# Moving one step of a VectorE exponential chain to GpSimd, with a third buffer, a longer look-ahead and a re-planned fixed schedule

## The chip, the cores and the metric

The kernel runs on one core of one Trainium2 chip. The metric is the device time of that core in microseconds (us). Executions of one kernel agree within about 0.8%, mostly within 0.4%, so each time below is a median of several runs. Every timed kernel ran beside the kernel before on the same chip. A ratio is the mean time of one kernel's fast runs over that of the kernel before's fast runs of the same rounds, with a 95% interval, so it is not quite the ratio of the medians quoted.

## The reference, cut to what matters

Two layers, each multi-query attention followed by a gated MLP. S = 2048, D = 512, 32 heads of 16, one K and one V for all heads.

```python
def _A_ref(x, wq, wk, wv, wo):
    q = (x @ wq) -> 32 heads of 16;  k = x @ wk;  v = x @ wv
    scores = jnp.einsum('bhqd,bkd->bhqk', q, k) * Dh ** (-0.5)
    p = _softmax(scores, axis=-1)                 # 2 layers x 32 heads x 2048 x 2048 exponentials
    o = jnp.einsum('bhqk,bkd->bhqd', p, v)
    return o @ wo
...
for _ in range(2):                                # written out in the original
    x = x + _A_ref(_layernorm(x), ...)
    x = x + _B_ref(_layernorm(x), ...)            # gelu, layernorm, spatial 2048x2048 product, gate, w_out
```

The exponentials dominate: two layers make 4096 score blocks of 128x512.

## The kernel before

The program is a list scheduler that runs at build time. Each operation has a planned duration, and the scheduler places operations one after the other on five engines. What it emits is only the *order* of each engine, plus semaphore waits for the data dependences. The planned start times are not part of the program: an engine runs its list in order, as soon as the inputs of the next entry are there.

```python
def op(self, eng, fn, dur, deps=(), prio=5.0, ...):   # dur: planned us, used only at build time
...
def emit_program(nc, es, sched):
    for o in sched.commits:
        ...
        for d in sorted(o.deps, key=lambda d: -d.vis):
            if o.eng == "pe" and d.eng == "pe":
                continue
            ...
            waits.append((d.sem.h, d.val))            # waits for data, not for time
        def body(e, waits=waits, fn=o.fn, h=s.h, incv=incv):
            for (h_, v_) in waits:
                e.wait_ge(h_, v_)
            fn(e).then_inc(h, incv)
```

A score block goes one of two ways. "A" blocks are exponentiated by ScalarE straight from PSUM. "D" blocks go to VectorE in batches of two (1024 columns): one step from PSUM to int32 for each block, then six steps on the batch in SBUF. Which block goes where is decided while the schedule is built.

```python
# DexStream.take: may VectorE take another block now?
if not self.batch:
    self.open = [o for o in self.open if o.start is None or o.end > t]
    if len(self.open) >= 2:
        return None
    backlog = sc.free["dve"] - t + sum(o.dur for o in sc.ready["dve"] if ...)
    if backlog > BACKLOG:                             # 3.0 us
        return None
...
# DexStream.chain: the six steps of a batch after the PSUM step
o2 = sc.op("dve", ts(u, lo, 2.0 ** -16, None), d_sb(n, 0.521e-3), self.ops, pr)   # u16 low half -> fp16
o3 = sc.op("dve", ts(w, u, None, -1.0), d_sb(n, 0.26e-3), [o2, getattr(self, "wfree", None)], pr)
o4 = sc.op("dve", lambda e: e.tensor_tensor(q, u, w, ALU.mult), d_sb(n, 0.521e-3), [o3], pr)
self.wfree = o4
o5 = sc.op("dve", ts(u, u, C_B, C_A), d_sb(n, 0.26e-3), [o4], pr)
o6 = sc.op("dve", lambda e: e.tensor_tensor(q, q, u, ALU.mult), d_sb(n, 0.521e-3), [o5], pr)
o7 = sc.op("dve", lambda e: e.scalar_tensor_tensor(po.bitcast(U16), I, 2.0 ** -9, q, op0=ALU.mult, op1=ALU.add),
           d_sb(n, 1.042e-3), [o6] + self.war, pr)    # writes the bits of the bf16 result
```

TensorE has one queue in one fixed order: score matmuls for both kinds of blocks, value matmuls, projections, and warm-up matmuls on zeros that keep it busy.

The softmax here doesn't subtract the row's maximum and nothing guards it: scores larger than these inputs give would overflow.

## Time and profile before

| | before |
|---|---|
| median of three runs | 1871.99 us (1869.53 to 1872.58) |
| profiled span | 1867.6 us |
| blocks on VectorE / ScalarE | 501 / 3595 |
| mean granted TensorE clock | 0.990 |

The page of the kernel before, its line of busy time (engine, busy us, share of the span, instructions) and its line of the chain of work that ended last:

```profile
PE 1595.0 (85%) x11889; PEld 477.3 (26%) x11889; DVE 1736.9 (93%) x3107; ACT 1756.6 (94%) x1581; POOL 53.4 (3%) x94
...
ACT 36%; DVE 30%; PE 18%; issue 14%; POOL 1%; ACTq 0%; POOLq 0%; DVEq 0%
```

PE is TensorE, DVE is VectorE, ACT is ScalarE and POOL is GpSimd. ScalarE and VectorE are both nearly full, the last chain runs through both, and GpSimd is idle. The table of windows of the same kernel (window in us; its length; for each engine busy us and instructions; granted clock; DMA share; GB/s) confirms this for two steady stretches:

```profile
100.00:150.00 50.00, 39.52 (x311) 9.88 (x307) 49.49 (x84) 49.94 (x45) 0.00 (x0) 0.98 0.00 1
1000.00:1050.00 50.00, 39.75 (x322) 10.17 (x314) 48.96 (x82) 50.00 (x46) 0.00 (x0) 1.00 0.00 1
```

VectorE (third) has 49.0 to 49.5 of 50 us, and ScalarE (fourth) 49.9 to 50.0. The costliest groups of the same page (line, engine, operation, output and input with shapes, count; then busy us, mean ns of one; then idle us before them and what ended it):

```profile
L1343 ACT ACTIVATE Pa<-ps_all 128x1536 bf16<-128x1536 f32 (+1 forms) x1439 | 1637.5, 1368 | 31.1 <-PE ps_all L1615 16.2
...
L1520 DVE TENSOR_SCALAR E<-ps_all 128x512 int32<-128x512 f32 x501 | 341.1, 683 | 28.8 <-PE ps_all L1615 26.3
...
L1558 DVE SCALAR_TENSOR_TENSOR Pd<-E 128x1024 uint16<-128x1024 int32 x251 | 304.4, 1213 | 1.1
...
L1553 DVE TENSOR_TENSOR E<-E 128x1024 f16<-128x1024 f16 x251 | 171.3, 682 | 3.4
L1556 DVE TENSOR_TENSOR E<-E 128x1024 f16<-128x1024 f16 x251 | 171.0, 681 | 2.5
L1547 DVE TENSOR_SCALAR E<-E 128x1024 f16<-128x1024 uint16 x251 | 171.1, 682 | 1.6
L1549 DVE TENSOR_SCALAR E<-E 128x1024 f16<-128x1024 f16 x251 | 104.5, 416 | 2.2
L1550 DVE TENSOR_SCALAR E<-E 128x1024 f16<-128x1024 f16 x251 | 104.3, 415 | 2.3
```

L1520 is the PSUM step, L1547 the low-half step `o2`, L1549 and L1550 are `o3` and `o5`, L1553 and L1556 `o4` and `o6`, L1558 is `o7`. The low-half step is 171 us of a full VectorE. ScalarE waits for score matmuls for only 16.2 us.

### The profile page before, as it was taken

Reading aid. Unit: us, or ns where it says so; the run is one execution under the profiler, and the core shown is the slowest. Engines: PE = TensorE matmul, PEld = TensorE weight load, DVE = VectorE, ACT = ScalarE, POOL = GpSimd, SP = SyncE. Lnnn points to the kernel's source line nnn. Section 1 sums busy time; section 2 is a strip of 40 time slices with the busy share of each in tenths; the row PEclk is TensorE's granted clock in tenths of the full one; section 3 lists DMA queues with packets and bytes.
Section 4 is the critical chain, followed back from the end, with each engine's and each line's share of the span. In section 5 each row is a group of like instructions: output and inputs, shape, how many; then the busy total and the mean of one; then the engine's idle time right before and its main releaser. Section 6 shows DMA issues by size and latency. Waiting matters only on the chain.

```text
span 1867.6 us, 30386 instructions
## 1 busy us (share of the span) xinstructions
PE 1595.0 (85%) x11889; PEld 477.3 (26%) x11889; DVE 1736.9 (93%) x3107; ACT 1756.6 (94%) x1581; POOL 53.4 (3%) x94
## 2 busy tenths in 40 slices
PE   8777888878889988989887778887788799999898
PEld 3222222212222222223432122222222222222234
DVE  8999999999879999997889999999999689989978
ACT  8999999999989999998579999999999899999983
POOL 2000000000000000000100000000000000000000
PEclk9999999999989999999999999999999899999999
DMA  9700010000010020221210000000000100111213
GB/s 272 197 1 1 12 35 1 1 1 18 7 40 24 23 46 1 66 70 48 66 33 1 1 1 12 10 26 1 5 13 7 40 24 24 46 43 35 62 45 110
DMA packets 125142, 68.58 MB, mean 37 GB/s; under 512 B 79172, under 2 KB 121416, under 8 KB 125000
## 3 DMA queue, kind: packets, MB, share of 16 engines
q1 hardware_dynamic: 123416, 66.48, 13.2%
q8 instruction: 95, 1.56, 0.3%
q14 instruction: 47, 0.39, 0.1%
q10 hardware_dynamic: 1584, 0.16, 0.1%
HBM read 30.97 MB, written 17.83 MB: 26 GB/s over the span
## 4 chain that ended last, share of the span: by engine, by line
ACT 36%; DVE 30%; PE 18%; issue 14%; POOL 1%; ACTq 0%; POOLq 0%; DVEq 0%
ACT Pa L1343 34%; PE ps_all L1088 6%; PE ps_all L1615 5%; DVE E L1520 5%; DVE Pd L1558 4%; PE ps_all L1419 3%; DVE E L1556 2%; DVE E L1553 2%; DVE E L1547 2%; DVE gp L1100 2%; PE ps_all L1177 1%; DVE st L622 1%; DVE E L1550 1%; DVE E L1549 1%; DVE z2n L937 1%
## 5 line engine op out<-in xcount | busy, mean ns | idle before, releaser
L1343 ACT ACTIVATE Pa<-ps_all 128x1536 bf16<-128x1536 f32 (+1 forms) x1439 | 1637.5, 1368 | 31.1 <-PE ps_all L1615 16.2
L1615 PE MATMUL ps_all<-qs,kT 32*128 32x512 bf16 x4096 | 566.5, 387 | 226.3 <-ACT Pa L1343 206.6
L1520 DVE TENSOR_SCALAR E<-ps_all 128x512 int32<-128x512 f32 x501 | 341.1, 683 | 28.8 <-PE ps_all L1615 26.3
L1615 PEld LDWEIGHTS ps_all<-qs,kT 32*128 32x128 bf16 x4096 | 139.3, 91 | 779.3 <-ACT Pa L1343 728.7
L1419 PE MATMUL ps_all<-Pa,V 128*32 128x512 bf16 x3595 | 324.9, 388 | 1.5 <-DVE Pd L1558 0.6
L1558 DVE SCALAR_TENSOR_TENSOR Pd<-E 128x1024 uint16<-128x1024 int32 x251 | 304.4, 1213 | 1.1
L1601 PE MATMUL ps_all<-zero 128*128 128x512 bf16 x817 | 263.3, 393 | 2.1 <-POOL zero L585 1.0
L1088 PE MATMUL ps_all<-wsT,z2n 128*128 128x512 bf16 x714 | 199.0, 383 | 6.5 <-DVE E L1520 2.6
L1419 PE MATMUL ps_all<-Pd,V 128*32 128x512 bf16 x501 | 177.7, 389 | 0.0
L1553 DVE TENSOR_TENSOR E<-E 128x1024 f16<-128x1024 f16 x251 | 171.3, 682 | 3.4
L1556 DVE TENSOR_TENSOR E<-E 128x1024 f16<-128x1024 f16 x251 | 171.0, 681 | 2.5
L1547 DVE TENSOR_SCALAR E<-E 128x1024 f16<-128x1024 uint16 x251 | 171.1, 682 | 1.6
L1549 DVE TENSOR_SCALAR E<-E 128x1024 f16<-128x1024 f16 x251 | 104.5, 416 | 2.2
L1550 DVE TENSOR_SCALAR E<-E 128x1024 f16<-128x1024 f16 x251 | 104.3, 415 | 2.3
L1601 PEld LDWEIGHTS ps_all<-zero 128*128 128x128 bf16 x817 | 62.7, 98 | 138.0 <-issue 116.8
L1419 PEld LDWEIGHTS ps_all<-Pa,V 128*32 128x32 bf16 x3595 | 65.3, 94 | 125.4 <-issue 114.3
L1100 DVE TENSOR_TENSOR gp<-ps_all,gp 128x512 f16<-128x512 f32 x112 | 75.0, 682 | 21.8 <-PE ps_all L1088 21.8
L1088 PEld LDWEIGHTS ps_all<-wsT,z2n 128*128 128x128 bf16 x714 | 54.5, 97 | 105.2 <-issue 54.8
L784 PE MATMUL ps_all<-xnTA,wq_pad 128*128 128x512 bf16 (+2 forms) x384 | 72.4, 313 | 2.0 <-DVE qs L793 1.3
L962 PE MATMUL ps_all<-xnTB,w_in_r 128*128 128x512 bf16 (+2 forms) x336 | 62.6, 310 | 5.2 <-DVE z1s L973 2.3
L926 PE MATMUL ps_all<-w_in_r,xnTB 128*128 128x448 bf16 x256 | 63.4, 356 | 3.5 <-DVE z2n L937 1.4
L1177 PE MATMUL ps_all<-E 128*128 128x512 bf16 x224 | 53.6, 380 | 4.2 <-ACT E L1156 3.6
(87 smaller groups left out, 1013.9 us busy)
## 6 DMA issues: line engine op xcount, KB each, us to landing
wsT_scratch<-gp SPq DMA_DIRECT2D x16, 512.0 KB, 3.6
wsT<-wsT_scratch SPq DMA_DIRECT2D x8, 1024.0 KB, 5.4
z1s<-z_scratch SPq DMA_DIRECT2D x16, 448.0 KB, 3.8
wsT<-wsT_scratch SPq DMA_DIRECT2D x8, 512.0 KB, 3.4
z_scratch<-z1s SPq DMA_DIRECT2D x4, 896.0 KB, 5.2
X<-in_A_x_dram SPq DMA_DIRECT2D x8, 256.0 KB, 5.3
out_dram<-X SPq DMA_DIRECT2D x16, 128.0 KB, 1.9
w_in_r<-in_B_w_in_dram SPq DMA_DIRECT2D x1, 1792.0 KB, 10.3
```

The source lines that it names most:

```text
L1088: ins = e.matmul(self.b32(b), self.z2n[:, s, f * 128:(f + 1) * 128], w_[:, s - s0, :], start=st, stop=sp)
L1343: return e.activation(k.Pa[:, base:base + n, :], k.b32(b0, n).rearrange("p (k q) -> p k q", k=n), ACTF.Exp, scale=SCALE)
L1419: ins = e.matmul(k.b32(k.pvb)[32 * j:32 * j + 32, :], k.V[:, u.kt, 32 * j:32 * j + 32], b.slot, tile_position=(0, 32 * j), start=u.first, ...
L1520: return k.sc.op("dve", lambda e: e.tensor_scalar(k.eI[:, s, 512 * i:512 * (i + 1)], k.b32(j.bank.idx)[:, 0:512], C_LOG2, C_BIAS, op0=ALU. ...
L1547: return lambda e: e.tensor_scalar(out, a, m, None, op0=ALU.mult)
L1549: return lambda e: e.tensor_scalar(out, a, b, None, op0=ALU.add)
L1550: return lambda e: e.tensor_scalar(out, a, m, b, op0=ALU.mult, op1=ALU.add)
L1553: o4 = sc.op("dve", lambda e: e.tensor_tensor(q, u, w, ALU.mult), d_sb(n, 0.521e-3), [o3], pr)
L1556: o6 = sc.op("dve", lambda e: e.tensor_tensor(q, q, u, ALU.mult), d_sb(n, 0.521e-3), [o5], pr)
L1558: o7 = sc.op("dve", lambda e: e.scalar_tensor_tensor(po.bitcast(U16), I, 2.0 ** -9, q, op0=ALU.mult, op1=ALU.add), d_sb(n, 1.042e-3), [o6] ...
L1601: return e.matmul(k.b32(k.pvb if b is None else b.idx), k.zero[:], k.zero[:, None, :].to_broadcast([P, 4, P]), start=b is not None, stop=b ...
L1615: return e.matmul(self.b32(bank), self.kT[32 * j:32 * j + 32, kt * 128:(kt + 1) * 128], self.qs[32 * j:32 * j + 32, g.q.slot, :], tile_pos ...
```

## The change

Its intent: give the low-half step to the idle GpSimd, and use the VectorE time that comes free for more blocks. GpSimd and VectorE can block each other (in the trace after, a VectorE step of 0.42 us then takes 1.26), so the new planner keeps their steps apart in its plan ("lock"). A third set of buffers covers the longer chain.

```diff
-LOOK = 6
+LOOK = 8
+PATIENCE = 3.0
+POOL_FREE = 1.0
...
-NQS = 6
+NQS = 4
...
+NDB = 3
...
-        o2 = sc.op("dve", ts(u, lo, 2.0 ** -16, None), d_sb(n, 0.521e-3), self.ops, pr)
-        o3 = sc.op("dve", ts(w, u, None, -1.0), d_sb(n, 0.26e-3), [o2, getattr(self, "wfree", None)], pr)
-        o4 = sc.op("dve", lambda e: e.tensor_tensor(q, u, w, ALU.mult), d_sb(n, 0.521e-3), [o3], pr)
-        self.wfree = o4
+        o2 = sc.op("pool", ts(u, lo, 2.0 ** -16, None), n * 0.93e-3 + 0.2, self.ops + [self.end[s]], 2.0)
+        o3 = sc.op("dve", ts(q, u, None, -1.0), d_sb(n, 0.26e-3), [o2], pr)
+        o4 = sc.op("dve", lambda e: e.tensor_tensor(q, u, q, ALU.mult), d_sb(n, 0.521e-3), [o3], pr)
...
+        for o in (o2, o3, o4, o5, o6, o7):
+            o.lock = True
...
-            if len(self.open) >= 2:
+            if len(self.open) >= NDB:
...
+    def unlocked(self, o, t, eng):                 # earliest start of a "lock" operation in the plan
+        t = max(t, self.locked["pool" if eng == "dve" else "dve"])
+        if eng == "pool" and self.free["dve"] < o.ready + PATIENCE:
+            d = self.order["dve"][-1]
+            free = max(0.0, d.end - t) if not d.lock else 0.0
+            free += sum(x.dur for x in self.ready["dve"] if x.eng == "dve" and not x.lock and x.ready <= t)
+            if free < POOL_FREE:
+                return INF
+        return t
...
+        pace = []                                  # warm-up matmuls wait for a recent operation
+        if t > k.sc.free["pe"] + 0.3:
+            pace = [d for en in ("act", "dve") for d in k.sc.order[en][-8:] if t - 1.5 < d.vis <= t]
+            pace = sorted(pace, key=lambda d: -d.vis)[:1]
...
-        self.onT = sb([P, 4, 4, 128], BF16, "onT")
+        self.onT = self.xnTB
```

The rest of it, cut here: one GELU batch less per layer, with the normalised half first; the transposes of one more chunk on TensorE; new priorities for late units and for the early spatial pass; a stream that places single score matmuls for VectorE. The planned duration of the GpSimd step at 1024 columns is 1024 x 0.93 ns + 0.2 us = 1.15 us.

## The prediction

> **What bounds the kernel now.** Two engines share the softmax exponentials: 3595 of the 4096 score blocks (128x512) go to ScalarE, 501 to VectorE, seven operations each. Busy time by windows of 50 us shows both saturated in steady stretches (ScalarE 49.9 to 50.0, VectorE 48.8 to 49.7). The page gives ScalarE 94%, VectorE 93%, GpSimd 3%. So the sum of both engines' work sets the time, as blocks can move between them. The rest is layer ends (880 to 957 us, and from 1803 us, with few exponentials) and the GELUs at 505 to 518 us, for which VectorE waits 9.5 us.
>
> **What the change removes, adds, moves.**
> - The low-half step (u16 to fp16, 128x1024, 682 ns, 251 times, 171 us in the groups of instructions) leaves VectorE for GpSimd. Back to back such operations start 0.60 us apart in the timeline, so about 0.31 us per block is saved of some 2.5.
> - GpSimd gets some 280 operations. It copied 128x1536 in 1464 ns, so I estimate 1.0 to 1.2 us each, and 340 to 390 us busy (19%).
> - The Trainium skill, page "SBUF — State Buffer", section "Who interferes with whom", says that GpSimd and a VectorE operation in a 2-port mode or with two SBUF inputs exclude each other for a whole instruction. The remaining five chain steps are of that kind; only the PSUM-reading first step (683 ns) and other evictions can run beside GpSimd. The trace of before shows no such overlap. The new schedule models this lock; two first steps just cover one GpSimd step. I estimate 0.2 to 0.3 us of VectorE stall per batch, 55 to 85 us in all. The third buffer hides the longer latency.
> - One GELU batch less per layer: two table loads of 1283 ns less, about 5 us of ScalarE in all; z2 is activated first, so statistics start some 6 us earlier, twice.
> - Transposes of chunk 4 move from DMA to TensorE, late projections and the early spatial pass get priority: a few us at each layer end, where gp additions now sit between the last chunk's steps.
>
> **How much is on the critical path.** Balance: ScalarE's other work and idle is 230 us plus 0.4555 us per block; VectorE's about 625 us plus 2.48 us per block (overlap taken off), falling to 2.17. Setting both equal gives 560 VectorE blocks and a span of 1841 us instead of 1867.6. By the same balance, a microsecond of VectorE stall costs 0.17 us and one of ScalarE saved gains 0.83 us. So lock stalls give back 9 to 14 us, table loads gain 4, layer ends and GELU order 5 to 12. Together about 1842 us, as a median of timed runs.
>
> Predicted: 1842 us, 8 in 10 between 1820 and 1864. Faster by over 2% (below 1834.5): 0.34; within 2%: 0.63; slower by over 2%: 0.03.
>
> **What would show each step.** Right: ScalarE's exponentials fall to about 1610 us; VectorE's first step rises to 550 to 565 counts; a GpSimd tensor-scalar of 128x1024 averages 1.0 to 1.2 us; ScalarE stays full in steady windows; VectorE's chain steps show 55 to 85 us of new idle or length beside GpSimd; two table loads less per layer. Wrong: the count stays near 500; the GpSimd step takes 2 us or more; ScalarE idles in steady windows for score matmuls.
>
> **What would make it wrong.** Mutual blocking much larger than planned, for order is fixed and actual times drift; GpSimd's reciprocal-root steps queueing behind exp steps; or layer ends that shrink by 10 us or more each, which brings it over 2%.

## More of the kernel before

`ts(out, a, m, b)` is a `tensor_scalar`. With only a factor or only a summand it has one arithmetic operation, and with both it has two.

## The result, and the profile after

The kernel after takes 2024.96 us (median of four, 2013.77 to 2029.55) beside 1872.28 us for the kernel before in the same rounds: ratio 1.0807 [1.0756, 1.0859]. It is 8% slower, where a small gain was predicted, and 2025 us lies far outside the predicted range.

| | before | after |
|---|---|---|
| median, us | 1872 | 2025 |
| blocks on VectorE | 501 | 531 |
| ScalarE's exponentials, busy us | 1637.5 | 1646.8 |
| ScalarE waits for score matmuls, us | 16.2 | 174.3 |
| mean TensorE clock | 0.990 | 0.924 |

The page of the kernel after, the same lines of it as before:

```profile
PE 1662.5 (82%) x11757; PEld 481.9 (24%) x11843; DVE 1826.5 (90%) x2966; ACT 1760.5 (87%) x1562; POOL 874.3 (43%) x356
...
DVE 60%; PE 23%; POOL 6%; ACT 6%; issue 5%; DMA 0%; POOLq 0%; ACTq 0%; DVEq 0%; SPq 0%
...
L1391 ACT ACTIVATE Pa<-ps_all 128x1024 bf16<-128x1024 f32 (+1 forms) x1427 | 1646.8, 1274 | 180.5 <-PE ps_all L1717 174.3
L1602 POOL TENSOR_SCALAR E<-E 128x1024 f16<-128x1024 uint16 x266 | 824.1, 3100 | 866.6 <-DVE E L1574 865.6
...
L1574 DVE TENSOR_SCALAR E<-ps_all 128x512 int32<-128x512 f32 x531 | 356.9, 680 | 50.3 <-PE ps_all L1717 49.0
L1612 DVE SCALAR_TENSOR_TENSOR Pd<-E 128x1024 uint16<-128x1024 int32 x266 | 338.4, 1272 | 1.8
...
L1608 DVE TENSOR_TENSOR E<-E 128x1024 f16<-128x1024 f16 x266 | 206.7, 778 | 3.9
...
L1610 DVE TENSOR_TENSOR E<-E 128x1024 f16<-128x1024 f16 x266 | 197.0, 741 | 3.3
...
L1604 DVE TENSOR_SCALAR E<-E 128x1024 f16<-128x1024 f16 x266 | 176.8, 665 | 38.1 <-POOL E L1602 38.1
L1605 DVE TENSOR_SCALAR E<-E 128x1024 f16<-128x1024 f16 x266 | 150.4, 566 | 3.2
```

L1602 is the low-half step, L1574 the PSUM step, L1604, L1608, L1605, L1610, L1612 are `o3` to `o7`. Four things can be read here.

1. The GpSimd step records 3100 ns on average. The planner had 1.15 us, and the prediction 1.0 to 1.2 us.
2. Every chain step on VectorE has become longer, though its shape is the same: `o3` from 416 to 665 ns, `o5` from 415 to 566, `o4` from 682 to 778, `o6` from 681 to 741, `o7` from 1213 to 1272. Only the PSUM step kept its length (683 and 680).
3. The differences times 266 add up to 66 + 40 + 26 + 16 + 16 = 164 us, and VectorE also waits 38 us for GpSimd. Together 202 us. This sum, called *VectorE's loss* below, is larger than the 171 us that left VectorE.
4. ScalarE has become a waiting engine: 174.3 us for score matmuls (L1717). The chain that ended last no longer runs through ScalarE (36% before, 6% after) but through VectorE (30% to 60%).

The timeline of the kernel after, VectorE and GpSimd around one step (start us, duration us, engine, line, operation; the time in brackets is idle time before it and what ended it):

```profile
126.11 1.21 DVE L1612 SCALAR_TENSOR_TENSOR Pd<-E 128x1024 uint16<-128x1024 int32 x1
126.27 3.67 POOL L1602 TENSOR_SCALAR E<-E 128x1024 f16<-128x1024 uint16 x1 [2.29 <-DVE E L1574]
127.24 1.26 DVE L1604 TENSOR_SCALAR E<-E 128x1024 f16<-128x1024 f16 x1
128.53 0.69 DVE L1608 TENSOR_TENSOR E<-E 128x1024 f16<-128x1024 f16 x1
129.25 0.97 DVE L1605 TENSOR_SCALAR E<-E 128x1024 f16<-128x1024 f16 x1
```

GpSimd starts 0.16 us after `o7` of another batch began. Its data were there, and nothing else holds it. This is no single case: counted over the whole trace, 188 of the 266 GpSimd steps begin while a chain step is running on VectorE. The plan had kept the two apart, but the emitted program doesn't. From 127.24 on, L1604 takes 1.26 us instead of 0.42, L1608 in the middle of the GpSimd step takes its ordinary 0.69, and L1605 takes 0.97 instead of 0.42.

How a slow VectorE reaches ScalarE can be seen in the waits of TensorE and ScalarE of the kernel after (engine, tile, line waiting; who it waits for; us in total, times, longest):

```profile
PE ps_all L1699 <- DVE E L1574: 18.2, 21, 2.2
PE ps_all L1717 <- DVE E L1574: 16.4, 24, 1.9
...
ACT Pa L1391 <- PE ps_all L1717: 174.3, 222, 4.1
```

TensorE's queue is in fixed order, and it stands at matmuls that wait for VectorE (a PSUM bank not yet read, or a warm-up matmul L1699 paced by a VectorE step) while the score matmuls that ScalarE needs stand behind them. The two lines on top are only the longest: summed over all lines of this view, TensorE waits 211 us for VectorE, against 47 in the kernel before. In the window of 100 to 150 us, where ScalarE had 49.94 us busy, it now has 44.28 (fourth engine), and the granted clock has gone from 0.98 to 0.86:

```profile
100.00:150.00 50.00, 39.14 (x280) 9.20 (x272) 48.99 (x70) 44.28 (x39) 28.82 (x10) 0.86 0.00 1
```

VectorE is as busy as before by the record, 48.99 us, though with 70 instructions instead of 84. Fewer were to be expected, as the low-half steps are gone, but a version below with the same order of instructions and hardly any blocking has 77 in 47.02 us. The record shows a blocked step as a longer busy one, so a busy share alone hides the effect.

### The profile page after: what moved, and what is told of

Its sections match the earlier page's. It is cut to its first block, busy times and chain, and to the rows that moved or that the text cites. A ratio compares the mean times of both kernels' runs of the same rounds, so it can differ in the third digit from the quotient of the medians.

```text
span 2027.7 us, 30245 instructions
## 1 busy us (share of the span) xinstructions
PE 1662.5 (82%) x11757; PEld 481.9 (24%) x11843; DVE 1826.5 (90%) x2966; ACT 1760.5 (87%) x1562; POOL 874.3 (43%) x356
## 4 chain that ended last, share of the span: by engine, by line
DVE 60%; PE 23%; POOL 6%; ACT 6%; issue 5%; DMA 0%; POOLq 0%; ACTq 0%; DVEq 0%; SPq 0%
DVE E L1574 11%; DVE Pd L1612 10%; DVE E L1608 7%; DVE E L1610 6%; PE ps_all L1717 6%; POOL E L1602 6%; DVE E L1604 6%; DVE E L1605 5%; ACT Pa L1391 5%; PE ps_all L1133 5%; PE ps_all L1467 4%; PE ps_all L1699 3%; DVE st L651 2%; DVE qs L822 1%; DVE oT L835 1%
## 5 line engine op out<-in xcount | busy, mean ns | idle before, releaser
L1391 ACT ACTIVATE Pa<-ps_all 128x1024 bf16<-128x1024 f32 (+1 forms) x1427 | 1646.8, 1274 | 180.5 <-PE ps_all L1717 174.3
L1602 POOL TENSOR_SCALAR E<-E 128x1024 f16<-128x1024 uint16 x266 | 824.1, 3100 | 866.6 <-DVE E L1574 865.6
L1717 PE MATMUL ps_all<-qs,kT 32*128 32x512 bf16 x4096 | 590.6, 410 | 166.9 <-ACT Pa L1391 124.3
L1574 DVE TENSOR_SCALAR E<-ps_all 128x512 int32<-128x512 f32 x531 | 356.9, 680 | 50.3 <-PE ps_all L1717 49.0
L1467 PE MATMUL ps_all<-Pa,V 128*32 128x512 bf16 x3565 | 352.5, 414 | 6.1 <-DVE oT L835 3.1
L1699 PE MATMUL ps_all<-zero 128*128 128x512 bf16 x755 | 270.9, 435 | 89.0 <-DVE E L1574 18.2
L1612 DVE SCALAR_TENSOR_TENSOR Pd<-E 128x1024 uint16<-128x1024 int32 x266 | 338.4, 1272 | 1.8
L1717 PEld LDWEIGHTS ps_all<-qs,kT 32*128 32x128 bf16 x4096 | 140.3, 92 | 739.2 <-ACT Pa L1391 554.4
L1604 DVE TENSOR_SCALAR E<-E 128x1024 f16<-128x1024 f16 x266 | 176.8, 665 | 38.1 <-POOL E L1602 38.1
L1608 DVE TENSOR_TENSOR E<-E 128x1024 f16<-128x1024 f16 x266 | 206.7, 778 | 3.9
L1467 PE MATMUL ps_all<-Pd,V 128*32 128x512 bf16 x531 | 199.4, 416 | 0.8 <-DVE Pd L1612 0.8
L1610 DVE TENSOR_TENSOR E<-E 128x1024 f16<-128x1024 f16 x266 | 197.0, 741 | 3.3
L1605 DVE TENSOR_SCALAR E<-E 128x1024 f16<-128x1024 f16 x266 | 150.4, 566 | 3.2
L1699 PEld LDWEIGHTS ps_all<-zero 128*128 128x128 bf16 x755 | 58.8, 101 | 238.9 <-issue 96.9
L657 POOL TENSOR_TENSOR rs<-ve,mhalf 128x2 f32<-128x2 f32 (+1 forms) x38 | 27.7, 730 | 91.4 <-DVE ve L655 78.5
```

Of the source, the lines that this page charges most:

```text
L1391: return e.activation(k.Pa[:, base:base + n, :], k.b32(b0, n).rearrange("p (k q) -> p k q", k=n), ACTF.Exp, scale=SCALE)
L1467: ins = e.matmul(k.b32(k.pvb)[32 * j:32 * j + 32, :], k.V[:, u.kt, 32 * j:32 * j + 32], b.slot, tile_position=(0, 32 * j), start=u.first, ...
L1574: c = k.sc.op("dve", lambda e: e.tensor_scalar(k.eI[:, s, 512 * i:512 * (i + 1)], k.b32(j.bank.idx)[:, 0:512], C_LOG2, C_BIAS, op0=ALU.mul ...
L1602: return lambda e: e.tensor_scalar(out, a, m, None, op0=ALU.mult)
L1604: return lambda e: e.tensor_scalar(out, a, b, None, op0=ALU.add)
L1605: return lambda e: e.tensor_scalar(out, a, m, b, op0=ALU.mult, op1=ALU.add)
```

## The experiments

The theories after the first reading were these:

- **T1, duration**: the GpSimd step is much longer than planned, and all follows from that.
- **T2, blocking**: the mutual blocking costs more than planned, because the order of the plan isn't held when the real times differ.
- **T3, the rest** (rival): the new look-ahead, third buffer, priorities and layer ends cost the time, and GpSimd little.
- **T4, clock** (rival): the paced warm-up matmuls let TensorE's clock fall, and slower score matmuls starve ScalarE.

### The step back on VectorE, all else kept

```diff
-        o2 = sc.op("pool", ts(u, lo, 2.0 ** -16, None), n * 0.93e-3 + 0.2, self.ops + [self.end[s]], 2.0)
+        o2 = sc.op("dve", ts(u, lo, 2.0 ** -16, None), d_sb(n, 0.521e-3), self.ops + [self.end[s]], pr)
```

> All of the change, but the low-half step back on VectorE. Theory A (the GpSimd step is the whole cause): 1850 to 1875 us, ScalarE full in steady windows, granted clock back at 0.97 to 1.0. Theory B (look-ahead, priorities, the paced warm-up matmuls or the shared transpose buffer cost the time): stays above 1950 us.

Measured: 2055.91 us, ratio 1.0978 [1.0954, 1.1002]. Taken alone this speaks for T3. But it is not the kernel after without GpSimd. With the planned VectorE work changed, the planner put 569 blocks on VectorE (531 before the edit), kept three batches open, and pushed other work to the end of a layer. The timeline of this run, a line of ScalarE at the end of the first layer (the time in brackets is the idle time before it and what ended it):

```profile
956.36 0.60 ACT L1204 ACTIVATE E<-ps_all 128x512 f16<-128x512 f32 x1 [41.56 <-PE ps_all L1192]
```

ScalarE stands 41.56 us at once for the layer's closing matmuls, and waits 171.9 us for them in the whole run. A likely reason is that the third buffer lets in batches for which VectorE has no room, so that its other work comes late. The next edit tests this by limiting the batches alone.

### The same with two open batches

```diff
-            if len(self.open) >= NDB:
+            if len(self.open) >= 2:
```

> The change with the step on VectorE (as in e1_low_on_dve) but at most two open exp batches, as in the kernel before. If e1 was slow because three open batches let exp work starve VectorE's other work, which then fell into the layer ends: 1850 to 1900 us and no hole on ScalarE after 895 us. If another part of the change is bad: over 1950 us.

Measured: 1857.03 us, ratio 0.9925 [0.9906, 0.9944], 493 blocks. ScalarE's wait for the closing matmuls fell from 171.9 to 27.6 us. The rest of the change is a gain of 0.75% without GpSimd, once the third batch is kept out. T3 falls as an explanation of the loss, and the first run's result is put down to the third batch on an overfull VectorE.

### The step on GpSimd alone, in the kernel before

```diff
-        o2 = sc.op("dve", ts(u, lo, 2.0 ** -16, None), d_sb(n, 0.521e-3), self.ops, pr)
+        o2 = sc.op("pool", ts(u, lo, 2.0 ** -16, None), n * 0.93e-3 + 0.2, self.ops, 2.0)
```

> The kernel before with one edit: the low-half step goes to GpSimd, planned at 1.15 us, two exp buffers, no lock in the schedule. Theory A (GpSimd step is the cause): slower than 1950 us, GpSimd step near 2.8 to 3.1 us, VectorE's 2-port steps lengthened by 150 us or more in all. Theory B (other parts): 1880 us or less. If it is slower than the kernel after, the third buffer and the modelled lock do help.

Measured: 2223.41 us, ratio 1.1888 [1.186, 1.1916]. VectorE waits 275.2 us for GpSimd, and its chain steps are some 90 us longer. The time lies where theory A put it, but the chain steps grew by less than the 150 us it named, and most of the loss is waiting. The loss comes with the move. All the other parts of the change together win back more than half of it; which of them does it this run doesn't tell.

### Telling the planner the real duration

```diff
-... n * 0.93e-3 + 0.2, self.ops + [self.end[s]], 2.0)
+... n * 2.6e-3 + 0.2, self.ops + [self.end[s]], 2.0)
```

> All of the change, but the build-time schedule is told that the GpSimd step takes 2.86 us (it measured 2.77 us undisturbed) instead of 1.15 us. Theory A1 (the loss is the surprise: an order made for a short step): most of it comes back, 1860 to 1930 us, ScalarE waits for score matmuls under 60 us. Theory A2 (the loss is the blocking itself, whatever the order): stays above 1970 us.

Measured: 1987.34 us, ratio 1.0619 [1.0579, 1.0659], 480 blocks. It is 38 us better than the kernel after and still 115 us worse than the kernel before: a wrong number in the plan is a part of it, not all. This lies between the theories and settles nothing alone.

### A quarter of the columns on GpSimd (wrong arithmetic on purpose)

The GpSimd step handles 256 of 1024 columns. The order of instructions on TensorE, VectorE and ScalarE is that of the kernel after. So that unwritten data can do no harm, the buffer is zeroed once at the start and `o5` multiplies by zero.

```diff
-        o2 = sc.op("pool", ts(u, lo, 2.0 ** -16, None), ...
+        o2 = sc.op("pool", ts(u[:, 0:n // 4], lo[:, 0:n // 4], 2.0 ** -16, None), ...
-        o5 = sc.op("dve", ts(u, u, C_B, C_A), d_sb(n, 0.26e-3), [o4], pr)
+        o5 = sc.op("dve", ts(u, u, 0.0, 0.001), d_sb(n, 0.26e-3), [o4], pr)
```

> Wrong result on purpose: same order of instructions on TensorE, VectorE and ScalarE as the kernel after, but GpSimd does 256 of the 1024 columns, so its step should take 0.7 to 0.9 us, less than was planned. Theory A (GpSimd's length and its blocking of VectorE are the cause): 1835 to 1865 us, granted clock over 0.97, chain steps on VectorE at their old lengths within 5%. Theory B (order and other parts of the change): 2000 us or more.

Measured: 1851.73 us, ratio 0.9900 [0.987, 0.9931]. The time is that of theory A; two details missed: the GpSimd step records 1.24 us on average instead of 0.7 to 0.9, and `o3` is 11% longer than before (461 and 416 ns), not within 5%. (The output comparison passed even so; it can't see an error of this size in the exponentials, so that it passes in other runs says little about them.) With the same order of instructions the loss is gone, so the order itself is good, and what GpSimd does while it runs makes the loss. The views by source line of this run (group, then min/median/max ns; first and last start) and its group of the GpSimd step:

```profile
L1604 DVE TENSOR_SCALAR E<-E x266: 284/418/625, 35.8 to 1761.8; 128x1024 f16<-128x1024 f16 x133
...
L1602 POOL TENSOR_SCALAR E<-E 128x256 f16<-128x256 uint16 x266 | 330.2, 1242 | 1164.5 <-DVE E L1574 1163.8
```

Even the worst `o3` is only 0.21 us longer than the median of 0.418.

### Warm-up matmuls without pacing

```diff
-        if t > k.sc.free["pe"] + 0.3:
+        if False:
```

> All of the change, same order, but the warm-up matmuls don't wait for ScalarE or VectorE work. Theory B1 (pacing stalls the TensorE queue and lets the clock fall): 1950 us or less, clock over 0.97. Theory A: within 1% of the kernel after, 2005 to 2045 us, as late VectorE work holds TensorE's queue anyway.

Measured: 2012.74 us, ratio 1.0748 [1.0727, 1.0769], mean clock 0.930 (0.924 with pacing). Its interval overlaps that of the kernel after, so a cost of the pacing isn't shown, and 0.6% (the difference of the ratios) is the most likely size if there is one. T4 falls: the clock stays low without the pacing, and below it rises from 0.951 to 0.980 in a run where only a wait of GpSimd was added. So here the clock follows the stalls and is not their origin. How much of the lost time passes through slower matmuls (a score matmul records 387 ns before and 410 after) isn't shown.

### A probe of GpSimd by itself

Nine GpSimd operations, twice, after the last store of the kernel before. VectorE and ScalarE are done by then, and in the second round, shown below, TensorE's warm-up matmuls are too:

```diff
+            for _ in range(2):
+                last = list(self.outs)
+                for fn in (
+                        lambda e: e.tensor_scalar(u, lo, m, None, op0=ALU.mult),        # the step itself
+                        lambda e: e.tensor_scalar(u[:, 0:512], lo[:, 0:512], m, None, op0=ALU.mult),
+                        lambda e: e.tensor_scalar(u, hi, m, None, op0=ALU.mult),        # dense u16
+                        lambda e: e.tensor_scalar(u, q, m, None, op0=ALU.mult),         # fp16
+                        lambda e: e.tensor_scalar(u, q, -1.0, None, op0=ALU.add),
+                        lambda e: e.tensor_scalar(u, q, m, 0.5, op0=ALU.mult, op1=ALU.add),
+                        lambda e: e.tensor_scalar(dst32, f32, m, None, op0=ALU.mult),
+                        lambda e: e.tensor_copy(u, q),
+                        lambda e: e.tensor_copy(u, lo)):                                # strided u16
+                    last = [sc.op("pool", fn, 2.0, last, 9.0)]
```

> The kernel before, and after its last store nine GpSimd operations, twice, with VectorE idle: the low-half step over 1024 and 512 columns, the same from dense u16, fp16 multiply, add, multiply-and-add, fp32 multiply, fp16 copy and u16-to-fp16 copy. If the step is slow by itself: 2.7 to 2.8 us for the first, half for 512. If the stride or the u16 conversion makes it slow: the dense or fp16 forms take 1.0 to 1.2 us. If blocking by VectorE made it slow: 1.0 to 1.2 us already for the first.

The timeline of the probe, GpSimd, in the order of the list above:

```profile
1886.45 2.77 POOL L1210 TENSOR_SCALAR E<-E 128x1024 f16<-128x1024 uint16 x1
1889.30 1.49 POOL L1211 TENSOR_SCALAR E<-E 128x512 f16<-128x512 uint16 x1
1890.87 2.77 POOL L1212 TENSOR_SCALAR E<-E 128x1024 f16<-128x1024 uint16 x1
1893.72 2.77 POOL L1213 TENSOR_SCALAR E<-E 128x1024 f16<-128x1024 f16 x1
1896.57 2.79 POOL L1214 TENSOR_SCALAR E<-E 128x1024 f16<-128x1024 f16 x1
1899.44 1.04 POOL L1215 TENSOR_SCALAR E<-E 128x1024 f16<-128x1024 f16 x1
1900.57 2.77 POOL L1216 TENSOR_SCALAR E<-E 128x1024 f32<-128x1024 f32 x1
1903.40 1.04 POOL L1217 COPY E<-E 128x1024 f16<-128x1024 f16 x1
1904.50 1.04 POOL L1218 CAST E<-E 128x1024 f16<-128x1024 uint16 x1
```

The step takes 2.77 us with nobody to block it. Neither the stride, nor the unsigned integers, nor the type makes it slow: every `tensor_scalar` of 1024 columns with *one* arithmetic operation takes 2.77 to 2.79 us, and the one with *two* (L1215) takes 1.04 us, as copy and cast do. The spacing of the starts agrees with the recorded lengths: 2.85 us from L1212 to L1213, 1.13 from L1215 to L1216. So the step can be about as short as the planner assumed, if it is written as "multiply and add zero". That makes two factors that can be set one by one: the form, and whether the start is held.

### The two-operation form, in the kernel after and in the kernel before

```diff
-        o2 = sc.op("pool", ts(u, lo, 2.0 ** -16, None), ...
+        o2 = sc.op("pool", ts(u, lo, 2.0 ** -16, 0.0), ...
```

> The kernel after, with the GpSimd step written as a multiply and an addition of zero, which the probe timed at 1.04 us instead of 2.77; same order on every engine, right result. If the slow form of one instruction is the whole cause: 1835 to 1860 us, GpSimd step 1.0 to 1.4 us, ScalarE's wait for score matmuls under 50 us, VectorE blocked under 60 us in all. If the order of the change is bad in itself: over 1950 us.

> The kernel before with only the step moved, in the fast form; two buffers, no lock in the schedule. If the move alone gives the gain: 1840 to 1860 us. If the modelled lock, the third buffer and the longer look-ahead are needed: 1870 to 1980 us, as VectorE runs into the lock unplanned.

Measured: in the kernel after, 1932.37 us, ratio 1.0328 [1.031, 1.0345]; in the kernel before with the step moved, 1959.2 us, ratio 1.0481 [1.046, 1.0503]. The form is worth 93 us in the kernel after (2025 to 1932) and 264 us in the kernel before (2223 to 1959). But 62 us remain to the kernel before, though the GpSimd step, undisturbed, is now no longer than planned, and the order of instructions is that of the kernel after. T1 alone is not enough. The view by source line and the timeline of the two-operation kernel after (GpSimd's step is on L1605 here):

```profile
L1604 DVE TENSOR_SCALAR E<-E x266: 284/417/1269, 35.8 to 1842.3; 128x1024 f16<-128x1024 f16 x133
...
121.40 1.21 DVE L1612 SCALAR_TENSOR_TENSOR Pd<-E 128x1024 uint16<-128x1024 int32 x1
121.57 1.95 POOL L1605 TENSOR_SCALAR E<-E 128x1024 f16<-128x1024 uint16 x1 [3.48 <-DVE E L1574]
122.54 1.26 DVE L1604 TENSOR_SCALAR E<-E 128x1024 f16<-128x1024 f16 x1
```

GpSimd again starts 0.17 us after an `o7` began, records 1.95 us instead of 1.04 because it is itself held up, goes on when `o7` ends, and now blocks the next chain step: 1.26 us instead of 0.42. The longest blocking is 1269 - 417 = 852 ns for 1024 columns, or 0.83 ns a column. With 256 columns (one-operation form) it was 625 - 418 = 207 ns, or 0.81 ns a column. In the kernel after no chain step was late by more than 845 ns either; but there 68 of the 266 GpSimd steps lengthened two chain steps by over 0.1 us each, and here none did.

### The plan without the lock

```diff
 for o in (o2, o3, o4, o5, o6, o7):
-    o.lock = True
+    o.lock = False
```

> e7_two_op with the schedule no longer told that the step and the chain exclude each other; buffers and look-ahead as in the change. If planning around the lock matters: 15 to 60 us slower than e7. If blocking by a 1.04 us step is cheap anyway: within 10 us of e7.

Measured, with the two-operation form: 1988.53 us, ratio 1.063 [1.0615, 1.0646], 544 blocks, against 1932 us and 531 blocks with the lock in the plan. Modelling the lock is worth 56 us even where the order alone carries it.

### The planned order held by a semaphore

GpSimd's step gets one more dependence: the last chain step that the plan put on VectorE ahead of it. The orders of instructions on TensorE, VectorE and ScalarE stay those of the kernel after.

```diff
         o.start = t
+        o.deps += [d for d in self.order["dve"] if d.lock][-1:] if o.lock and eng == "pool" else []
```

> e7_two_op, same order on every engine, but each GpSimd step also waits for the VectorE chain step that the schedule put last before it, so that it starts where it was planned, beside PSUM-reading steps. If e7 is still slow because nothing holds GpSimd to its planned slot (in its trace the step starts 0.16 us after a chain step begins and then holds up the next one by 0.86 us): 1835 to 1855 us, chain steps within 5% of their old lengths, ScalarE waits under 40 us. If the blocking comes anyway: within 1% of e7, 1913 to 1951 us.

> The kernel after with the same hold, but the slow form of the step (2.77 us). If early start is the larger half of the loss: 1900 to 1940 us. If the slow form is what hurts: 1980 us or more, as a 2.77 us step outlasts any slot planned for 1.15 us.

Measured: with the two-operation form 1859.14 us, ratio 0.9941 [0.9922, 0.996]: 4 us above the expected range, with the chain steps and ScalarE's wait as expected. With the one-operation form 2087.11 us, ratio 1.1155 [1.1141, 1.117]: the second of its two forecasts. The timeline of the held kernel with the two-operation form:

```profile
128.54 1.22 DVE L1612 SCALAR_TENSOR_TENSOR Pd<-E 128x1024 uint16<-128x1024 int32 x1
129.67 0.68 DVE L1574 TENSOR_SCALAR E<-ps_all 128x512 int32<-128x512 f32 x1
129.84 1.05 POOL L1605 TENSOR_SCALAR E<-E 128x1024 f16<-128x1024 uint16 x1 [7.20 <-DVE Pd L1612]
131.10 0.69 DVE L1574 TENSOR_SCALAR E<-ps_all 128x512 int32<-128x512 f32 x1 [0.75 <-PE ps_all L1717]
131.71 0.42 DVE L1604 TENSOR_SCALAR E<-E 128x1024 f16<-128x1024 f16 x1
```

Now GpSimd starts after `o7`, runs 1.05 us beside the PSUM steps, and `o3` takes its old 0.42 us. This is what the plan had meant. Over the whole trace, 17 of the 266 GpSimd steps begin inside a chain step, where it was 196 without the hold, and TensorE's waits for VectorE fall from 147 to 57 us. The page of that run, busy time and the groups of `o3` and `o7`:

```profile
PE 1577.0 (85%) x11757; PEld 473.5 (26%) x11843; DVE 1675.8 (90%) x2966; ACT 1737.6 (94%) x1562; POOL 344.3 (19%) x356
...
L1612 DVE SCALAR_TENSOR_TENSOR Pd<-E 128x1024 uint16<-128x1024 int32 x266 | 329.9, 1240 | 1.8
...
L1604 DVE TENSOR_SCALAR E<-E 128x1024 f16<-128x1024 f16 x266 | 111.1, 418 | 20.2 <-POOL E L1605 19.8
```

With the slow form the hold hurts: the GpSimd step, longer than the room the plan left for it, starts later, and VectorE waits. The waits of VectorE in that run:

```profile
DVE E L1604 <- POOL E L1602: 211.2, 159, 2.9
```

Five kernels with the same order of instructions on those three engines form a series (compared instruction by instruction, their traces agree). VectorE's loss is worked out as above: mean minus the mean of before, times count, summed over the five chain steps, plus the wait for GpSimd.

| kernel after with | VectorE's loss, us | ScalarE's wait for score matmuls, us | median, us |
|---|---|---|---|
| nothing changed | 163.6 + 38.1 = 201.7 | 174.3 | 2025 |
| one-operation form, held | 27.7 + 211.2 = 238.9 | 222.3 | 2087 |
| two-operation form | 124.2 + 0 = 124.2 | 86.5 | 1932 |
| two-operation form, held | 13.3 + 19.8 = 33.1 | 29.2 | 1859 |
| a quarter of the columns | about 21 | 24 | 1852 |

From the fourth line to the third the loss grows by 91 us and the time by 73 us; to the first by 169 and 166 us; to the second by 206 and 228 us. So a microsecond of loss costs 0.8 to 1.1 us of time, not 0.17.

### The right duration, held

```diff
-... n * 0.93e-3 + 0.2, self.ops + [self.end[s]], 2.0)
+... n * 0.83e-3 + 0.19, self.ops + [self.end[s]], 2.0)
```

This plans 1.04 us, as the probe measured for the two-operation form.

> e11_two_op_held with the step planned at 1.04 us instead of 1.15. If the over-long plan costs blocks: over 535 VectorE blocks and 1845 to 1855 us. If the lock itself takes the gain: within 5 us of e11.

Measured: 1850.14 us (1845.85 to 1851.46), ratio 0.9874 [0.9857, 0.9891], result correct. This is the fastest version here. It beats both kernels, the kernel before by 1.26%. It isn't by more blocks, which was the reason given for trying it: VectorE has 526, where 531 were with the longer plan. ScalarE's time outside busy (span minus busy) fell from 118.5 to 104.3 us, mostly at layer ends (its wait for the keys' matmuls alone fell from 17.9 to 8.1 us). Its window (columns as before) shows a full ScalarE, and a VectorE with 3.7 us to spare:

```profile
100.00:150.00 50.00, 39.23 (x304) 9.69 (x305) 46.26 (x75) 50.00 (x45) 10.46 (x9) 0.97 0.00 1
```

### Two attempts to use the spare time

The first lets more work wait for VectorE, the second lets GpSimd start with less lock-free VectorE work in sight.

```diff
-BACKLOG = 3.0
+BACKLOG = 5.0
```

> e13 with the limit on queued VectorE work at 5 us instead of 3. If admission holds VectorE back: over 540 blocks, 1840 to 1855 us. If more exp work only starves the other work (as in e1_low_on_dve): slower than e13 by 5 us or more.

```diff
-POOL_FREE = 1.0
+POOL_FREE = 0.5
```

> e13 with the GpSimd step allowed to start when only 0.5 us of lock-free VectorE work is queued, instead of 1.0. If waiting for a slot costs more than a short block: 1845 to 1855 us. If blocking costs more: VectorE's chain steps lengthen by 30 us or more in all, and the time is over 1862 us.

Measured: 1859.41 us, ratio 0.9929 [0.9905, 0.9953], 530 blocks; and 1863.2 us, ratio 0.9956 [0.9935, 0.9978], 535 blocks. The first is 9 us slower than 1850, as its second forecast said, though starved work was not looked for. The second is over 1862 us, but its chain steps lengthened by 22 us in all, not 30. Both have more blocks on VectorE, and both are slower than 1850. So a higher count isn't worth anything in itself, and why the schedule leaves VectorE some 4 of 50 us idle stays open. Nor does blocking explain why the two are slower: VectorE's loss, worked out as above, is 35 us at 1850, 31 at 1859 and 34 at 1863. Each new constant makes the planner place everything anew, and with equal loss the times still spread over 13 us.

## Why the prediction was wrong

It was wrong in direction: about 1842 us was predicted, 2025 measured. Its readings of the kernel before held. Four steps of its sum failed.

**"It copied 128x1536 in 1464 ns, so I estimate 1.0 to 1.2 us each" failed.** The step takes 2.77 us undisturbed. A copy is not the same operation as a one-operation `tensor_scalar`. In the probe, copy and cast take 1.04 us for 1024 columns, just as estimated, and the one-operation form 2.77. The Trainium skill, page "GPSIMD Engine Reference", section "4.1 Engine selection", calls one-input elementwise work on GpSimd "roughly line-rate". The trace agrees for the two-operation form, copy and cast (1.04 us, about 1.0 ns a column), and not for the form that the change used (2.77 us, about 2.7 ns a column). Changing the form alone took 2025 to 1932 us. Why the one-operation form is slow no run shows.

**"I estimate 0.2 to 0.3 us of VectorE stall per batch, 55 to 85 us in all" failed.** It was 202 us, or 0.76 us a batch. Some 78 us of it went with the form of the step. Another 91 us went when the start was held, in this order only: holding the slow form raised the loss by 37 us. The prediction took the plan's word: "The new schedule models this lock; two first steps just cover one GpSimd step". A planned start is no start on the chip. In the traces GpSimd starts when its inputs are there (188 of 266 times inside a chain step), goes on when the chain step that runs ends, and blocks the next one for up to 0.85 us. With the start held by a semaphore, the loss went from 124 to 33 us and the time from 1932 to 1859. The prediction named this risk ("order is fixed and actual times drift"), but gave it almost no weight: 0.03 for slower.

**"A microsecond of VectorE stall costs 0.17 us" failed.** It cost about 1 us (166 us of time for 169 us of loss). The 0.17 assumes that blocks move to ScalarE when VectorE slows down. They do so while the plan is made, and only for what the plan knows. A stall that the plan doesn't know meets a fixed split and a fixed order on TensorE, and the score matmuls that ScalarE needs stand behind matmuls that wait for VectorE. TensorE's waits for VectorE rose from 47 to 211 us and ScalarE's for score matmuls from 16 to 174; with the loss they fell to 57 and 29. ScalarE's exponentials, forecast to fall to about 1610 us, stood at 1646.8.

**"560 VectorE blocks" failed.** It was 531, and 526 to 535 in the better variants. The balance of engine sums left out that the plan lets GpSimd start only beside lock-free work; with the lock out of the plan the count was 544. What else in the planner limits it isn't shown.

The parts that held: two table loads less per layer (21 loads to 17, 1283 ns each); the rest of the change is a small gain, 0.75% with the step on VectorE and two open batches. The page cited in the prediction, "SBUF — State Buffer", section "Who interferes with whom" of the Trainium skill, says that such VectorE steps and GpSimd exclude each other, and that a step with at most one SBUF input outside the 2-port modes does not. The traces agree on which steps: the PSUM step keeps 680 to 684 ns in every run, and all five others grow in the kernel after. They agree less on "for the whole instruction". Within the recorded 3.67 us of one GpSimd step, L1608 ran at its ordinary 0.69 us, between two stalls of 0.84 and 0.55 us.

Of the three signs named in advance for a failure two came: the GpSimd step over 2 us, and ScalarE idle in steady windows for score matmuls. The third, a count near 500, did not (531). With both faults mended the best version is 1.26% faster than the kernel before, at 1850 us, 8 us from the predicted number and within its range. That nearness is luck: it has 526 blocks and not 560, and a version without GpSimd's step reaches 1857 us (0.9925). Whether the move itself is worth anything isn't shown. Of the four versions that hold the two-operation step, one (0.9874) is faster than the version with the step on VectorE, and the other three (0.9929, 0.9941, 0.9956) are not; planner constants alone spread the times by more than the half per cent that would be the gain.

What stays open: why the one-operation form takes 2.77 us; why the slow form blocks in pieces; why the schedule doesn't fill VectorE; whether GpSimd's step is a gain at all once it is short and held; and how much of the last 9 us (1859 to 1850) is the shorter plan and how much the chance of another order.

## What to carry to other kernels

Measure the very instruction that you want to move, on the engine it moves to, in its exact form: here a second arithmetic operation (add zero) made it 2.7 times faster. A build-time schedule holds only what semaphores hold, so where two engines exclude each other, make the planned order a dependence, and only after the step has its planned length: held with the slow form, the kernel became slower still. An unplanned stall in an engine of a statically split load cost about its full length here, so don't discount it by the balance that the planner could have found. And where every edit makes a planner order everything anew, compare several orders before calling a half per cent a gain.

## What the Trainium skill lacked or had wrong

- "GPSIMD Engine Reference", section "4.1 Engine selection", doesn't tell forms of one-input work apart. For 1024 columns, a `tensor_scalar` with one arithmetic operation took 2.77 to 2.79 us (fp16, u16 and fp32; multiply or add; strided or dense), with two 1.04 us, and copy and cast 1.04 us.
- "SBUF — State Buffer", section "Who interferes with whom", has the block last for the whole instruction. With the one-operation form no chain step was late by more than 0.845 us, and within one recorded GpSimd step of 3.67 us a VectorE chain step ran at its ordinary 0.69 us between two stalls.
- The same section gives the length of a block only as the whole instruction, with no figure. Here it was up to 852 ns for 1024 columns and 207 ns for 256 columns of the GpSimd step, or about 0.8 ns a column.
- It also doesn't say how the profile shows a block: here as a longer busy time of the blocked VectorE step (1.26 us in place of 0.42), not as idle time.
